# Another order of the same steps in a planned RWKV-7 and SwiGLU kernel

## The chip, the core and the metric

The kernel runs on one core of one Trainium2 chip. The metric is device time in microseconds (us). The kernel before was run three times: 1099.3, 1105.6 and 1111.4 us, median 1105.6. One further execution was recorded by the hardware profiler; it took 1106.7 us from its first to its last instruction, and all figures of the profile are of that one.

## The reference

Two blocks follow each other. The first is a linear recurrence over 768 steps of a sequence, for 4 batches of 8 heads of width 40, each with a state of 40 x 40:

```
for t in range(S):
    y[:, :, t] = einsum('bhd,bhde->bhe', rt, state)
    Sa = einsum('bhde,bhe->bhd', state, at)
    state = state * wt[:, :, None, :] - einsum('bhd,bhe->bhde', Sa, bt) \
            + einsum('bhd,bhe->bhde', vt, kt)
```

The second takes the recurrence's output as 3072 tokens of width 320, divides each by its root mean square, scales it by `rms_g`, and applies a SwiGLU layer:

```
g, val = xn @ w_gate, xn @ w_val          # 320 x 1536 each
out = (g * sigmoid(g) * val) @ w_out      # 1536 x 320
```

The weights come as 64-bit floating point numbers and are used as fp32.

## The kernel before, in words

**Chunks.** The recurrence is cut into 24 chunks of 32 steps. `front(c)` (line 678) loads a chunk (`wan`, `kbn`, `VU`, `wn`), turns it over on PE (the tensor engine), and builds over the levels 1 to 16 the products of keys and decays (`K`, `Ab`, `KN`) and the chunk's triangular matrix `LT`. `LT` is written to `sB` in device memory and read back into `M` in another layout. `inverse(c)` (line 782) inverts it by 31 pairs of DVE (vector engine) steps, `tmp<-Yi,M` and `Yi<-Yi,tmp`, each of which needs the one before. The result goes to `sY` in device memory and back into `LT`. `main(c)` (line 802) uses `LT` in two `lower` products, updates the state `ST`, computes the chunk's output `y` level by level (`As`, `level`, `down`), and turns it into a column block of `xg`, the normalized input of the second block.

**Groups.** Two chunks make a group of 64 steps. `feed(g)` (line 924) is the SwiGLU layer for such a group of 256 tokens, with 12 slices of weights taken in six pairs. For each pair SP (the sync engine) loads two `wf` tiles, PE makes the products `h64` and `h`, ACT (the scalar engine) makes `sg`, DVE makes `hT`, and PE adds `out` into the PSUM tile `po`. ACT then copies `po` to `o`, and SP stores it. There are 12 groups.

**Weights.** `narrow` (line 958) turns the weights' 64-bit numbers into fp32 on DVE and ACT, once, and stores them in `sW`, from which all groups load. It runs beside the first chunks.

**Order.** Nothing is issued while these functions run. Each call of a helper (`dve` at line 473, `scalar` at 492, `dma` at 516, `pe` at 526) records a step in a `Plan`, with what it needs; a PE step is a whole product of up to 64 matmuls. When all is recorded, `Plan.issue` (line 347) walks through a written list, `ORDER`. A number in it picks a recorded step, counted from the first one that is not yet issued; a `-` issues one filler matmul (line 1002), which multiplies the identity by itself into an unused part of `po` to keep PE's clock up:

```
for word in order.split():
    if word == "-":
        self.order.append(None)
        self.warm()
        continue
    i = first + int(word)
```

So `ORDER` sets the sequence of steps on each of the five engines, DMA issues included: SP and GpSimd (POOL) issue loads in that sequence, and a load that must wait for its buffer holds up those behind it. `PAIRS` gives each of the 491 PSUM uses ("rooms") one of three pairs of banks. Waits between engines follow from the recorded needs and from the reuse of buffers and banks.

All steps of a helper bear that helper's line in the profile: L475 is nearly all of DVE, L521 all matmuls of products, L524 the turns, L518 all DMA issues, L502 ACT's copies, L1002 the filler. They are told apart by their tiles.

Of the kernel before, what the change touches and what calls it, by code (L numbers as in the profile page):

```python
# [16 lines left out]
P = 128  # L17
# [10 lines left out]
PRODUCTS = {  # L28
    "out": (0.915, 0.359, 0.434, 0, 2560), "h": (1.618, 0.306, 0.381, 0, 4096), "h64": (0.864, 0.2, 0.2, 1, 2048),
    "turn": (0.824, 0.2, 0.273, 0, 2048), "turn3": (0.278, 0.3, 0.275, 0, 768), "turn4": (0.388, 0.249, 0.272, 0, 1024),  # L30
    "turny": (0.46, 0.145, 0.248, 2, 640), "gram": (0.927, 0.124, 0.264, 2, 512), "gramk": (0.927, 0.158, 0.263, 2, 1792),
    "score": (0.927, 0.138, 0.243, 2, 1024), "level": (0.603, 0.132, 0.216, 5, 1024), "state": (0.597, 0.126, 0.245, 3, 640),
    "lower": (0.594, 0.126, 0.216, 4, 320), "update": (0.603, 0.154, 0.265, 2, 1280), "y0": (0.613, 0.132, 0.236, 2, 1024),
}

LOADS = {
    "sB": (1.75, 0.1), "LT": (2.0, 0.2), "M": (2.67, 0.44), "sY": (1.96, 0.3), "wf": (4.02, 1.46), "r": (4.25, 0.69),
    "tok": (2.09, 0.27), "wn": (2.36, 0.31), "wan": (2.68, 0.51), "out": (1.9, 0.15), "g": (2.37, 0.68),
    "raw2": (3.1, 0.75), "raw64": (2.21, 0.27), "rawo": (2.9, 0.7), "rawp": (2.4, 0.3), "sW": (1.5, 0.7),
}  # L40
# [5 lines left out]
36 33 2 26 42 1 31 0 25 343 37 29 107 38 24 36 26 34 262 2 13 1 35 40 0 190 24 339 13 14 - - - 40 17 44 15 41 43 55  # L46
42 8 60 47 175 72 48 45 84 185 59 68 186 585 54 58 - - - - - 49 93 586 53 179 69 71 599 81 176 57 597 50 67 178 609
70 188 80 622 51 92 16 623 65 610 52 56 177 633 64 66 - - - - - - - - - - - - 61 189 9 598 77 79 187 78 587 620 62 0
587 81 - - - - 72 75 179 82 62 90 595 384 194 588 87 11 633 89 589 74 395 620 197 590 380 88 73 195 391 - - - - 101
196 209 390 610 84 102 214 381 201 611 202 5 212 86 213 383 591 85 0 222 92 591 611 17 95 221 224 223 384 94 234 225  # L50
- - 197 233 237 93 391 245 246 592 328 393 198 598 645 612 0 641 598 15 612 592 - 338 205 206 380 642 599 209 0 207
612 200 0 337 612 186 598 6 326 613 2 599 641 34 176 200 216 217 23 600 389 215 33 201 355 95 202 177 96 214 - - - -
211 187 339 93 0 577 0 561 578 297 579 171 192 53 187 191 - - - 182 188 200 623 172 185 625 186 580 562 581 612 355
582 199 1065 197 583 611 183 198 624 184 0 152 1005 850 298 0 298 0 837 295 0 0 0 83 130 298 148 0 298 83 0 507 307
833 0 303 555 0 840 307 0 290 0 67 125 316 314 0 132 125 67 0 0 131 314 0 286 325 0 130 0 298 130 0 291 292 - - - -
- 287 0 293 0 304 0 316 305 301 0 0 283 0 296 0 311 0 322 281 0 286 0 295 280 0 292 - - - - - - - - - - - - - - - -
- 288 0 0 0 0 301 0 285 62 301 116 305 0 283 250 116 0 - - - - - - - - 293 0 258 112 296 0 110 300 256 0 308 307 245
293 292 0 0 304 0 288 0 301 - - - - - - 298 306 0 0 313 0 297 0 0 0 293 310 494 301 0 494 0 302 0 0 299 492 0 0 296
0 246 0 791 0 0 0 787 0 0 93 468 2 796 94 469 0 94 462 794 0 467 93 94 290 461 95 462 96 468 511 97 469 291 98 470
481 289 99 292 471 0 99 100 101 471 102 472 103 481 511 104 482 105 488 106 489 107 483 2 490 108 109 0 293 109 490  # L60
0 108 0 0 379 0 379 387 0 387 369 0 405 378 387 406 0 - - - - - - - - - - - - - - - - - - - - - - - - - - - - - - -
- - - - - - - - - - - - - - - - - - - - - - - - - - - - - - - - - - - - - - - - 44 0 367 377 0 415 0 42 0 414 383 43
412 0 383 410 0 383 40 373 0 0 0 0 0 0 36 0 377 - - - - - - - - - - - - - - - - - 44 0 377 35 44 0 414 0 0 82 0 32 -
43 0 373 0 90 0 229 407 38 88 0 40 78 226 42 38 41 47 48 0 43 226 42 50 45 48 396 0 50 396 43 0 396 0 0 379 395 380
0 395 380 0 401 0 394 0 378 242 400 44 0 400 47 0 145 45 377 242 0 145 391 377 0 216 1 145 391 42 635 398 429 626
146 0 397 39 145 426 634 398 146 147 631 43 623 44 621 45 632 46 148 47 622 - - - - 639 375 376 149 48 416 239 641
830 150 399 377 640 840 0 150 641 653 48 838 151 658 152 645 828 - - - - - - 642 153 670 154 646 155 682 49 656 50
156 669 657 51 157 666 158 667 52 159 643 668 - - - - - - - 53 389 160 161 678 162 1 651 652 - 647 2 702 655 3 654 0
594 610 611 609 625 595 636 109 608 110 596 373 - - - - - - - - - - - 605 590 374 111 345 783 607 626 782 383 112
627 620 622 385 793 113 623 606 375 382 114 792 621 - - - - - - - 617 384 115 376 346 116 377 619 117 635 634 118  # L70
618 378 119 - - - - - 160 633 120 379 121 163 380 161 122 381 123 162 124 164 386 - - - - - - - - - 629 125 387 126
127 128 388 129 630 130 640 631 389 638 131 390 - - - - - 167 641 132 391 133 639 134 392 168 135 393 - - - - - 165
136 394 137 138 430 139 166 571 431 581 643 140 - - - 171 721 644 580 141 642 142 570 143 174 645 144 173 145 178 -
- - 182 175 146 177 147 172 150 149 179 - - - 180 148 637 176 185 732 432 186 433 0 1065 584 283 - 39 1064 36 582 38
284 638 37 40 635 583 0 17 635 480 625 567 497 40 18 624 498 41 284 568 626 42 285 499 627 43 570 286 642 636 44 500
2 706 287 45 643 897 0 493 500 501 643 287 897 656 644 648 2 45 597 907 502 649 494 0 457 860 458 0 613 0 457 611
552 0 - 596 457 621 598 0 622 0 456 595 610 853 457 622 458 634 854 0 505 - - - 500 360 765 521 361 449 531 519 764
504 532 543 362 508 363 0 500 517 543 501 4 515 363 502 364 506 419 514 365 5 366 516 367 0 367 419 368 421 369 370
420 422 44 0 370 - 430 371 44 0 3 40 0 367 426 368 369 370 504 371 37 372 373 374 375 429 376 526 525 521 377 505
522 0 338 466 390 339 397 377 9 340 391 341 392 342 430 393 398 343 480 440 400 378 439 395 387 429 396 394 403 408  # L80
388 0 403 0 342 474 700 403 578 0 700 403 342 709 490 343 0 474 7 696 405 343 709 475 403 344 0 487 706 472 0 485
695 10 343 704 404 0 404 0 4 404 37 405 0 401 31 337 481 402 45 0 474 3 337 338 41 339 402 0 42 3 0 398 705 399 471
50 335 400 898 336 703 470 401 337 37 907 338 339 402 27 480 699 908 704 340 403 341 897 479 486 701 889 343 700 584
478 890 713 714 481 899 702 719 28 706 559 900 342 712 29 560 731 30 0 531 9 0 9 683 684 17 10 0 10 454 0 450 552 10
451 0 10 672 0 672 - - - - - - - - - - - - - - - - 662 25 0 27 670 26 0 682 680 24 695 539 677 676 678 704 661 37 -
- - - 3 36 675 662 296 4 681 434 691 663 679 692 703 672 5 0 0 428 1 680 683 42 682 666 43 687 681 667 20 40 686 21
677 695 2 22 292 0 675 705 287 0 675 287 688 0 671 0 669 665 269 7 17 410 8 682 29 411 412 30 667 413 414 0 8 665 0
675 8 681 672 9 674 0 9 672 - - - - - - - - - - 481 0 9 37 483 411 0 471 0 25 5 401 6 402 403 404 471 7 39 405 473 -
- - - - - - - - - - - 16 0 0 28 8 27 397 0 397 28 0 397 0 654 462 0 5 396 36 8 397 398 37 399 14 47 462 15 0 457 10
723 44 3 11 43 458 583 644 21 12 646 582 4 13 645 461 0 571 21 13 572 458 393 22 14 394 15 466 0 391 455 19 0 372 0  # L90
16 436 0 694 28 5 27 442 6 695 371 439 7 0 696 0 451 370 435 6 760 0 745 0 428 0 741 362 425 0 751 433 362 741 0 748
362 0 425 423 358 733 0 358 0 744 358 432 359 360 0 427 428 0 7 359 0 359 15 0 359 360 6 0 425 0 428 442 359 360 361
362 363 364 0 360 361 742 362 0 362 363 364 419 365 742 366 367 2 368 423 751 369 370 371 372 373 424 675 374 7 0
424 2 0 1154 672 0 1154 421 422 732 432 738 0 669 730 1002 732 670 420 995 731 439 742 685 985 421 0 993 421 687 735
422 686 743 4 1002 423 748 736 991 424 746 983 366 757 367 759 368 425 992 369 744 0 369 746 371 757 755 370 759 768
# [155 lines left out]
02120120011200000212212111011122220122021022212000000011220202110212200222211102110020200221100000001111122201220111  # L251
201121210102011022201201201
"""


class Piece:

# [136 lines left out]
def kernel(  # L394
# [41 lines left out]
    N = 8  # L436
# [98 lines left out]
    ident = const.tile([P, P], FP32, name="ident")  # L535
# [499 lines left out]
```

## Time and profile before

| What | Value |
|---|---|
| median of 3 runs | 1105.6 us |
| profiled execution, span | 1106.7 us |
| PE busy, filler included | 1032.9 us (93%) |
| filler alone | 75.7 us, 560 records |
| DVE busy | 907.4 us (82%), 3065 instructions |
| ACT busy | 453.9 us (41%) |
| POOL busy | 302.7 us (27%) |
| DMA | 145.4 MB, 131 GB/s on average |
| granted PE clock, mean | 0.984 |

Busy time is the union of an engine's instructions. The row of PE holds matmuls only; weight loads overlap them and have a row of their own. A row of a group of instructions gives their number, busy time, mean duration in ns, and the idle time of the engine just before them with what ended it. A row of the waits gives who waited for whom, the total in us, how often, and the longest. A row of DMA issues gives the KB of each and the median time from issue to landing in us. A row of a stretch gives its bounds and length in us, then for each engine the busy time and, in brackets, the instructions.

### The profile page before, as it was taken

The numbers are of one execution on the slowest core, as the hardware profiler recorded it, in microseconds if no ns is written. First come the engines' busy times: TensorE is split into PE (matmuls) and PEld (weight loads), VectorE is DVE, ScalarE is ACT, GpSimd is POOL, SyncE is SP. The second block draws the span as 40 slices with busy tenths as digits, with TensorE's granted clock in tenths as the row PEclk, the third lists the DMA queues.
The fourth block names the chain that finished last, engine by engine and source line by source line (L and its number), as shares of the span: only waits on it lengthen the run. The fifth ranks groups of instructions, "written<-read, shape, count | busy, mean of one in ns | idle before, by whom it ended". The sixth has DMA issues, their size and how long they took to land.

```text
span 1106.7 us, 53122 instructions
## 1 busy us (share of the span) xinstructions
PE 1032.9 (93%) x23152; PEld 852.5 (77%) x23152; DVE 907.4 (82%) x3065; ACT 453.9 (41%) x989; POOL 302.7 (27%) x534
## 2 busy tenths in 40 slices
PE   5697888989999999999999999999989999999998
PEld 4597877767778877877777877887878878787876
DVE  5998999799889888798789789988898889798421
ACT  3644544654244344344344345334335435332211
POOL 7520342122233223223323323413404312200000
PEclk9789899989999999999999999999999999999999
DMA  7545453786555536456535545645636546434242
GB/s 158 134 85 164 122 125 85 198 240 165 124 141 124 149 80 160 117 125 141 150 101 138 138 123 134 154 101 151 139 95 166 125 112 147 108 108 131 80 141 80
DMA packets 171177, 145.43 MB, mean 131 GB/s; under 512 B 123712, under 2 KB 142080, under 8 KB 170944
## 3 DMA queue, kind: packets, MB, share of 16 engines
q1 hardware_dynamic: 152576, 119.06, 39.8%
q0 software_dynamic: 16192, 22.64, 11.0%
q8 instruction: 182, 2.98, 1.2%
q10 hardware_dynamic: 2176, 0.33, 0.2%
q14 instruction: 51, 0.42, 0.1%
HBM read 125.83 MB, written 16.12 MB: 128 GB/s over the span
## 4 chain that ended last, share of the span: by engine, by line
PE 59%; DVE 19%; issue 7%; ACT 3%; DMA 3%; POOL 2%; SPq 0%; DVEq 0%; POOLq 0%; ACTq 0%
PE ps L521 41%; PE po L521 11%; PE ps L524 7%; DVE LT L475 3%; DVE tmp L475 3%; DVE Yi L475 2%; DVE As L475 2%; DVE y L475 2%; DVE K L475 1%; DVE hT L475 1%; DVE r L475 1%; DVE ex L475 1%; DVE wf L475 1%; ACT K L502 1%; DMA sB<-LT 1%
## 5 line engine op out<-in xcount | busy, mean ns | idle before, releaser
L521 PE MATMUL ps<-xg,wf 128*128 128x256 f32 (+1 forms) x1728 | 354.5, 392 | 3.1 <-DVE xg L475 2.1
L521 PEld LDWEIGHTS ps<-xg,wf 128*128 128x128 f32 (+1 forms) x1728 | 261.3, 189 | 58.4 <-issue 14.3
L521 PE MATMUL po<-wf,hT 128*128 128x320 f32 x576 | 178.8, 444 | 3.2 <-DVE hT L475 1.8
L475 DVE TENSOR_TENSOR tmp<-Yi,M 128x60 f32<-128x60 f32 (+24 forms) x744 | 156.0, 210 | 18.1 <-DMA M<-sB 1.9
L475 DVE TENSOR_TENSOR Yi<-Yi,tmp 128x60 f32<-128x60 f32 (+24 forms) x744 | 155.3, 209 | 15.9
L518 POOL DMA_DIRECT2D VU<-in_v_dram x92 | 53.4, 587 | 356.6 <-PE ps L524 206.3
L498 ACT ACTIVATE sg<-ps 128x256 f32<-128x256 f32 x144 | 53.7, 383 | 236.4 <-PE ps L521 225.0
L521 PEld LDWEIGHTS po<-wf,hT 128*128 128x128 f32 x576 | 102.2, 190 | 39.3 <-issue 3.7
L475 DVE TENSOR_TENSOR hT<-ps,sg 128x256 f32<-128x256 f32 x144 | 59.3, 419 | 54.7 <-ACT sg L498 53.4
L475 DVE TENSOR_TENSOR K<-K,T 128x512 f32<-128x512 f32 (+1 forms) x192 | 93.4, 495 | 8.7 <-PE ps L521 3.4
L521 PEld LDWEIGHTS ps<-Ab,K 40*64 40x64 f32 x4608 | 76.6, 137 | 30.8 <-issue 9.6
L521 PE MATMUL ps<-Ab,K 40*64 40x56 f32 x4608 | 86.4, 223 | 11.5 <-DVE K L475 3.1
L502 ACT COPY K<-K 128x256 f32<-128x256 f32 (+1 forms) x168 | 71.2, 443 | 61.9 <-PE ps L521 40.6
L475 DVE TENSOR_TENSOR As<-ps,msi 128x256 f32<-128x256 f32 (+1 forms) x192 | 83.2, 481 | 10.6 <-PE ps L521 10.4
L502 ACT COPY KN<-ps 128x640 f32<-128x640 f32 x96 | 66.4, 691 | 53.4 <-PE ps L524 20.7
L521 PEld LDWEIGHTS ps<-As,KN 128*40 128x40 f32 x3072 | 67.2, 125 | 19.5 <-issue 11.7
L521 PE MATMUL ps<-As,KN 128*40 128x32 f32 x3072 | 74.5, 206 | 7.3 <-issue 4.6
L1002 PE MATMUL po<-ident 128*128 128x128 f32 x560 | 75.7, 291 | 5.3 <-ACT po L544 5.3
L1002 PEld LDWEIGHTS po<-ident 128*128 128x128 f32 x560 | 70.4, 203 | 6.7 <-POOL wan L514 5.2
L518 POOL DMA_DIRECT2D kbn<-in_b_dram x92 | 53.6, 586 | 78.5 <-PE ps L521 70.8
L518 POOL DMA_DIRECT2D wn<-in_w_dram x92 | 51.5, 566 | 85.9 <-DVE tmp L475 32.4
L518 POOL DMA_DIRECT2D kbn<-in_k_dram x92 | 53.4, 584 | 75.7 <-PE ps L521 75.0
(124 smaller groups left out, 1529.2 us busy)
## 6 DMA issues: line engine op xcount, KB each, us to landing
wf<-sW SPq DMA_DIRECT2D x144, 480.0 KB, 4.2
M<-sB SPq DMA_DIRECT2D x96, 128.0 KB, 3.9
rn<-in_r_dram SPq DMA_DIRECT2D x24, 160.0 KB, 4.3
sW<-ex SPq DMA_DIRECT2D x16, 240.0 KB, 4.0
out_dram<-o SPq DMA_DIRECT2D x48, 80.0 KB, 3.5
kbn<-in_b_dram POOLq DMA_DIRECT2D x92, 40.0 KB, 3.2
wan<-in_w_dram POOLq DMA_DIRECT2D x46, 80.0 KB, 3.9
wan<-in_a_dram POOLq DMA_DIRECT2D x46, 80.0 KB, 4.3
```

The source lines that it names most:

```text
L475: plan.add("DVE", time + more + each * size(o), 0.087, lambda at: fn(at(o), *m(at)), [o], aps(*args))
L498: scalar(o, [a], lambda at: nc.scalar.activation(at(o), at(a), f, **kw), aps(acc), 0.1 if f in (AF.Square, AF.Relu) else 0.0)
L502: scalar(o, [a], lambda at: nc.scalar.copy(at(o), at(a)), extra=more)
L518: plan.add(by, 0.6 if by == "POOL" else 0.45, 0.0, lambda at: queue.dma_start(out=o, in_=i), [o], [i], load=LOADS[load], since=since)
L521: return o, lhsT, rhs, lambda at: nc.tensor.matmul(at(o), lhsT, rhs, start=start, stop=stop, skip_group_check=True), 4
L524: return o, i, ident, lambda at: nc.tensor.transpose(at(o), i, ident), 2
L1002: plan.warm = lambda: nc.tensor.matmul(po_[:, 0, DM:DM + P], ident, ident, start=False, stop=False, skip_group_check=True)
```

## The change

`ORDER` and `PAIRS` are replaced. The same steps with the same tiles and operands are issued in another sequence, found anew by exchanging steps along the chain that ends last: 3,043 on DVE, 968 on ACT, 897 on PE, 712 on SP and 507 on POOL. A DVE step moves by 16 places at the median and by 257 at most. 315 of the 491 rooms lie in another PSUM pair. The number of fillers goes from 280 to 235. The tables `PRODUCTS` and `LOADS`, which held durations for the planner and took no part in the issue, are gone, and with them their uses; a PE step records its kind instead, and one kind of turn gets a name of its own.

```
-PRODUCTS = {
-    "out": (0.915, 0.359, 0.434, 0, 2560), "h": (1.618, 0.306, 0.381, 0, 4096), "h64": (0.864, 0.2, 0.2, 1, 2048),
...
-LOADS = {
-    "sB": (1.75, 0.1), "LT": (2.0, 0.2), "M": (2.67, 0.44), "sY": (1.96, 0.3), "wf": (4.02, 1.46), "r": (4.25, 0.69),
...
 ORDER = """
-36 33 2 26 42 1 31 0 25 343 37 29 107 38 24 36 26 34 262 2 13 1 35 40 0 190 24 339 13 14 - - - 40 17 44 15 41 43 55
...
+36 27 3 26 37 1 346 345 0 184 26 17 39 29 21 37 36 2 3 27 44 12 38 6 28 194 108 183 45 46 182 51 190 52 - - - - 48
...
-        plan.add(by, 0.6 if by == "POOL" else 0.45, 0.0, lambda at: queue.dma_start(out=o, in_=i), [o], [i], load=LOADS[load], since=since)
+        plan.add(by, 0.6 if by == "POOL" else 0.45, 0.0, lambda at: queue.dma_start(out=o, in_=i), [o], [i], load=load, since=since)
...
-        time, drain, tail, mode, area = PRODUCTS[kind]
-        plan.add("PE", time, tail, issue, [s[0] for s in steps] + more, [x for s in steps for x in s[1:3]],
-                 drain=drain, mode=mode, area=area, many=sum(s[4] for s in steps))
+        plan.add("PE", 0.0, 0.0, issue, [s[0] for s in steps] + more, [x for s in steps for x in s[1:3]],
+                 kind=kind, many=sum(s[4] for s in steps))
...
-        pe("turn", [flip(ps[0:outs, at(n), 0:ins], t[0:ins, n, 0:outs], ident[0:ins, 0:ins]) for n in range(N)])
+        pe("turn" if ins == P else "turnS", [flip(ps[0:outs, at(n), 0:ins], t[0:ins, n, 0:outs], ident[0:ins, 0:ins]) for n in range(N)])
```

## The prediction

> **What bounds the kernel now.** I read the busy time by stretches first. I cut the span where feed group 0 starts (165 us), where group 1 starts (270) and where the last group starts (1060).
>
> ```profile
> core 0: us, PE busy (x) PEld busy (x) DVE busy (x) ACT busy (x) POOL busy (x), PEclk, DMA share, GB/s
> 0.00:165.00 165.00, 129.85 (x2860) 118.90 (x2864) 142.21 (x469) 82.04 (x162) 67.80 (x134) 0.92 0.56 132
> 165.00:270.00 105.00, 93.91 (x2023) 76.95 (x2013) 94.26 (x294) 55.01 (x111) 26.30 (x45) 0.97 0.62 169
> 270.00:1060.00 790.00, 767.90 (x18093) 625.61 (x18092) 665.52 (x2293) 311.37 (x705) 208.60 (x356) 1.00 0.51 128
> 1060.00:1107.00 47.00, 41.28 (x192) 30.99 (x192) 5.46 (x13) 5.44 (x14) 0.00 (x0) 0.98 0.37 111
> ```
>
> PE looks busy throughout, but part of it is the filler matmul of L1002, which does no work. The same two first stretches for that line alone:
>
> ```profile
> 0.00:165.00 165.00, 65.05 (x474) 60.24 (x474) 0.92 0.56 132
> 165.00:270.00 105.00, 10.64 (x86) 10.14 (x86) 0.97 0.62 169
> ```
>
> Taking filler off, PE works 64.8 of the first 165 us, 83.3 of the next 105, 767.9 of the next 790. It loses 100, 22, 22 and 6 us: two thirds before the first feed step. There DVE is the busy one: it starts its first planned step at 14.9 us, and from then to 165 its idle stretches longer than 0.12 us add up to 8.1 us. So **the first 270 us go by DVE, the 790 us behind them by PE**, and a new order can gain most in front.
>
> Next the order in time of DVE, in the middle stretch (start, duration, instruction):
>
> ```profile
> 337.56 0.19 DVE L475 TENSOR_TENSOR tmp<-Yi,M 128x35 f32<-128x35 f32 x1
> 337.78 0.20 DVE L475 TENSOR_TENSOR Yi<-Yi,tmp 128x35 f32<-128x35 f32 x1
> 338.01 0.19 DVE L475 TENSOR_TENSOR tmp<-Yi,M 128x28 f32<-128x28 f32 x1
> 338.12 0.41 DVE L475 TENSOR_TENSOR y<-y,ps 128x256 f32<-128x256 f32 x1
> 338.56 0.42 DVE L475 TENSOR_TENSOR y<-y,T 128x256 f32<-128x256 f32 x1
> ```
>
> A step that reads what its neighbour just wrote starts after it has ended (337.56 + 0.19 = 337.75, next at 337.78). A step that doesn't starts before (338.01 + 0.19 = 338.20, next at 338.12). Over all 1,168 dependent neighbours of this trace the median gap is +0.035 us, over the 1,874 others -0.082. **Two dependent DVE steps side by side cost 0.117 us more than the same two apart.**
>
> **The change, part by part.** No instruction goes but filler: 3,043 DVE, 897 PE, 968 ACT, 712 SP and 507 POOL steps stand in both lists.
>
> *PE's own work.* With each step at its median start-to-start time behind that kind, by the next kind, the sum is 942 us in the old order and 940 in the new. I cost it at 0.
>
> *Filler.* 280 become 235; at 0.27 us each (75.7 us for 560 records, two to a filler) that is 12.2 us less. They stood where PE had nothing else, so 0 by themselves. If PE then idles and its clock falls (it was granted 0.92 in the first stretch), the 64.8 us of work there grow; at 0.80 by 64.8 x (0.92/0.80 - 1) = 10 us. I take 0, since DVE ends last there, and keep 10.
>
> [...]
>
> *DVE's order.* Counting dependent neighbours in the two built lists gives 1,168 before and 792 after. 376 x 0.117 = 44 us of DVE time go. What that is worth depends on the place. I summed, in order, the duration of each DVE step's form, plus 0.035 or minus 0.082 by its neighbour, up to four points, and the PE work standing ahead of the PE step that uses the result. Where DVE sets the pace, the time won is the fall in DVE ahead, less what PE has done less by then:
>
> - group 0 starts: DVE 134.7 to 123.7 (100 dependent neighbours become 38: 7.3 us, and 3.7 us of work less ahead), PE ahead 59.5 to 58.4: 11.0 - 1.1 = 9.9 us
> - group 0, third weight pair: DVE 174.8 to 154.3, PE 90.8 to 84.3: 14.0 us
> - group 0, last weight pair: DVE 222.7 to 216.1, PE 129.2 to 136.5: 6.6 + 7.3 = 13.9 us
> - group 1 starts: DVE 227.5 to 209.5 (178 dependent become 52), PE 137.7 to 130.6: 10.9 us
>
> The four are alike, mean 12.2. **I take -12 us up to 270 us.** The ends are -18 (all of the DVE fall) and 0 (the loads are late instead).
>
> [...]
>
> *The middle.* DVE's sum per group falls from 72.6 to 69.6 us, against 81 us that a group takes, so DVE isn't the bound there. What can go is PE's 22 us of idle. PE's waits from 300 to 1060 us:
>
> ```profile
> PE ps L521 <- issue: 5.5, 12, 1.3
> PE ps L521 <- DVE LT L475: 3.0, 5, 1.4
> PE ps L521 <- ACT KN L502: 1.5, 4, 0.6
> PE ps L521 <- DVE xg L475: 1.5, 2, 1.0
> PE ps L524 <- DVE tmp L475: 1.3, 2, 0.9
> ```
>
> The rows that name DVE add up to 8.5 us. I take two thirds, **-6 us**, since new places of steps also make new waits; the ends are 0 and -22. The last product for the state (main 23, 0.75 us), whose result nobody reads, now stands behind everything, beside the copy of `o` (0.69 us) and the last store: 0.
>
> *Round trips through SP.* The inverse leaves the core and comes back (`sY`, then `LT`); the step that waits is `lower` on PE, with the rest of that chunk behind it.
>
> ```profile
> wf<-sW SPq DMA_DIRECT2D x144, 480.0 KB, 4.2
> ...
> LT<-sY SPq DMA_DIRECT2D x96, 32.0 KB, 2.9
> ```
>
> In the trace, from the last `Yi` to the landing of the last `LT` it took 9.9 us at best (chunk 23), 15.5 at the median, when the order left time. The old order has at least 14.0 us of PE work in that place from chunk 2 on. The new one has 9.4 (chunk 2), 9.1 (3), 11.2 (4), 10.0 (14), 11.2 (17) and 7.1 (23). At 9.9 us the shortfall is 0.5 + 0.8 + 2.8 = **+4 us**, which I take, because the SP queue need not carry the slack it carried. The ends are 0 and, at 15.5 for all 22 chunks, +43. Loads of `wf` with under 6 us of cover rise from 6 to 17 of 144; 4.2 us is their median landing: 0. The trip of `LT` to `M` gets shorter too (7.7 us of PE work at chunk 13, where the fastest start of an inverse came 10.2 us behind `LT`), but DVE waits there, with 11 us to spare per group: 0, and up to 2 us a chunk if PE runs dry.
>
> **Sum:** -12 - 6 + 4 = -14 us on the execution of 1106.7 us: 1092.7. The runs' median lies 1.1 us below that execution, so 1091.5.
>
> **The rivals.**
>
> *No gain.* The order was found against costs that the chip doesn't have, and where DVE leaves off ACT or a load is late: DVE waited 9.6 us for ACT's copy of `T` at the start already. Then the 12 us shrink to 4 or less and the new waits take that back: 1106.7 - 4 + 4, about 1106.
>
> *Slower: the round trip of the inverse.* `lower` stands at the head of PE's queue, so each late `LT` stops everything. If a trip takes 14 us in the new order, the shortfalls are 4.6 + 4.9 + 2.8 + 4.0 + 2.8 + 6.9, and 1.2 in two further chunks: 27 us. With the 12 won in front and nothing in the middle: 1106.7 - 12 + 27 = 1122. From about 12 us a trip it takes back what was won (14 us); from some 13.5 the kernel is over 1% slower. For it: landings spread up to 5 us at the ninth decile. Against it: 9.9 was reached.
>
> *A larger gain.* DVE's 18 us count in full and most of the 22 in the middle go: 1106.7 - 18 - 18 + 1 = 1072.
>
> **How the numbers follow.** Forecast (1080 to 1098) 0.47, larger gain 0.12, no gain 0.26, slower 0.15. A measurement of this kernel tells about 1%, 11 us (its runs spread from 1099 to 1111). Below 1094.5 lie the larger gain and most of the forecast: 0.56; within 0.29; slower 0.15. Half of the larger gain (0.06) and nearly all of the slower case (0.13) are left out: 1072 to 1114.
>
> **What would show it.** Right: the first step of feed group 0 starts near 155 us and group 1 near 258; DVE has some 790 neighbours with the longer gap; PE idle from there to the last group is below 20 us; 470 filler records. Wrong: PE waits named after `LT<-sY` of over a microsecond in many chunks, group 0 still at 165, or a lower clock in front with PE on the chain.

## The result, and the profile after

The changed kernel takes 1204.3 us (median of four runs, 1193.9 to 1205.7) against 1104.2 us (1099.3 to 1111.4) for the kernel before: a ratio of 1.088, 95% interval 1.082 to 1.094. It is 8.8% slower where a gain of about 1% was forecast. The profiled execution takes 1203.6 us with a span of 1201.8 us.

First the busy time by stretches of the changed kernel, cut where its groups 0, 1 and 11 start. The columns are those shown of the kernel before: bounds, length, busy time of PE, its weight loads, DVE, ACT and POOL, granted clock, DMA share, GB/s.

```profile
core 0: us, PE busy (x) PEld busy (x) DVE busy (x) ACT busy (x) POOL busy (x), PEclk, DMA share, GB/s
0.00:150.00 150.00, 117.04 (x2777) 108.22 (x2778) 132.19 (x451) 77.72 (x156) 65.55 (x129) 0.95 0.56 140
150.00:257.00 107.00, 90.89 (x1971) 72.56 (x1969) 85.70 (x278) 53.23 (x107) 25.41 (x42) 0.90 0.55 149
257.00:1153.00 896.00, 803.79 (x18058) 644.52 (x18060) 648.35 (x2327) 303.86 (x712) 214.50 (x363) 0.97 0.44 115
1153.00:1202.00 49.00, 43.47 (x260) 31.95 (x258) 4.81 (x12) 5.78 (x14) 0.00 (x0) 0.98 0.36 113
```

The front is shorter, as forecast. The long stretch behind it took 790 us before and takes 896 now, and PE, with as many instructions in it (18,058 against 18,093), is busy 36 us longer there and idle 70 us longer. Its clock, 1.00 before, is 0.97. DVE does the same work in less time (665.5 before, 648.4 now).

Next PE's waits of the changed kernel from 300 us to the last group: what it waited for, total us, how often, the longest.

```profile
PE ps L522 <- issue: 26.6, 23, 4.4
PE ps L522 <- DVE hT L476: 8.9, 14, 1.7
PE po L522 <- DVE hT L476: 8.4, 7, 2.4
PE ps L522 <- DVE tmp L476: 7.1, 4, 3.9
```

Two things are new beside the rows shown of before. "Issue", a wait for nothing that the profile shows, was 5.5 us with 1.3 at the longest; now it is 26.6 with 4.4. And PE waits for `hT`, DVE's step of the feed, which was not among its five largest waits. The loads did not take longer from issue to landing (4.2 and 2.9 us before):

```profile
wf<-sW SPq DMA_DIRECT2D x144, 480.0 KB, 3.9
...
LT<-sY SPq DMA_DIRECT2D x96, 32.0 KB, 2.9
```

**What an "issue" wait is.** In the order in time of PE it lies in the middle of a product, where nothing is handed over. This is one product of 64 matmuls of the changed kernel (start, duration, instruction, number of them, and in brackets the idle time ahead):

```profile
356.28 0.90 PE L522 MATMUL ps<-A,K 40*64 40x56 f32 x43
361.55 0.89 PE L522 MATMUL ps<-A,K 40*64 40x56 f32 x21 [4.37 <-issue]
```

I counted PE's instructions (matmuls, weight loads, and the waits on semaphores that stand between them) from the start of the trace. Nearly all of these stalls sit where the count leaves 193 when divided by 256, in every run of this study. The queue q8, of the kind "instruction" in the page, moved 181 packets of 16,384 bytes in this trace, in which I count 46,432 instructions of PE, and 182 in that of before, with 46,625: one packet for 256 instructions. I read this as PE at the end of a piece of its code while the next piece is not there yet: the packet ahead of the stall above started at 358.6 us and took 1.5 us, and PE went on 1.5 us after it had landed. In all traces the fetch of a piece started when PE had at most 297 instructions left (the median is about 177), took about 1.1 us, and the first instruction ran at least 1.1 us after it landed (1.3 to 1.5 us in the 28 stalls of this trace behind 270 us). By estimate from the rows of this trace, 256 instructions of PE last some 28 us in `h` products (two of them, 32 instructions, in 3.5 us) but 2.3 us in products of `Ab` and `K` (128 in 1.16 us). I call these stalls **late code**.

The table gives, for each kernel, group starts from the traces and two sums behind 270 us: stalls of more than 0.15 us at these boundaries, and the time in which PE's granted clock was at half ("half clock"). At half clock the `h` matmuls of the changed kernel stood 0.43 us apart, start to start at the median of 16, and 0.22 us at full clock. "`sg` late" sums, over the 144 `sg` steps, the time from the end of the product it reads to its start.

| kernel | time, us | group 0 | group 1 | group 2 | group 11 | late code, us (number) | half clock, us | `sg` late, us |
|---|---|---|---|---|---|---|---|---|
| before | 1104.2 | 165.5 | 270.1 | 346.2 | 1060.6 | 8.7 (16) | 3 | 62 |
| after | 1204.3 | 150.5 | 257.3 | 362.4 | 1152.7 | 34.1 (28) | 55 | 193 |
| front1 | 1139.8 | 154.1 | 276.0 | 353.1 | 1095.7 | 19.8 (24) | 30 | 73 |
| rest1 | 1215.3 | 163.1 | 267.3 | 357.8 | 1163.4 | 37.5 (33) | 75 | 174 |
| noM | 1189.3 | | | | | 33.4 (28) | 44 | 189 |
| noall | 1220.5 | 157.9 | 265.0 | 364.7 | | 43.2 (36) | 80 | 186 |
| noW | 1168.4 | 150.5 | 256.6 | 356.8 | 1117.5 | 15.1 (18) | 33 | 190 |
| noWB | 1098.3 | | | | | 2.0 (4) | 2 | 62 |
| shiftA | 1218.6 | 161.4 | 264.7 | 364.9 | 1167.4 | 40.7 (35) | 64 | 188 |
| shiftB | 1153.9 | 165.4 | 271.5 | 353.5 | 1106.0 | 30.9 (28) | 46 | 62 |
| shiftB256 | 1112.8 | 168.3 | 274.3 | 350.5 | 1064.8 | 9.8 (16) | 4 | 61 |
| shiftBW | 1134.7 | 166.0 | 273.3 | 352.0 | 1086.6 | 14.3 (17) | 36 | 62 |
| front1fix | 1113.6 | 149.7 | 273.7 | 349.9 | 1063.4 | 7.4 (14) | 3 | 75 |
| front1fill | 1115.8 | 152.8 | 278.0 | 354.1 | 1067.9 | 7.8 (14) | 2 | 73 |
| adjB | 1137.7 | 161.6 | 269.4 | 349.8 | 1088.2 | 11.3 (17) | 15 | 152 |
| early | 1208.3 | 151.8 | 258.1 | 363.5 | 1157.6 | 32.6 (32) | 50 | 114 |

The kernel before took 1103 to 1106 us (medians) beside every group of runs. Where no interval is given, a kernel was run once.

### The profile page after: what moved, and what is told of

It reads as the page before. It is cut to its first block, busy times and chain, and to the rows that moved or that the text cites. A ratio compares the mean times of both kernels' runs of the same rounds, so it can differ in the third digit from the quotient of the medians.

```text
span 1201.8 us, 52799 instructions
## 1 busy us (share of the span) xinstructions
PE 1055.2 (88%) x23062; PEld 857.2 (71%) x23062; DVE 871.1 (72%) x3065; ACT 440.6 (37%) x989; POOL 305.5 (25%) x534
## 5 line engine op out<-in xcount | busy, mean ns | idle before, releaser
L522 PE MATMUL ps<-xg,wf 128*128 128x256 f32 (+1 forms) x1728 | 363.7, 401 | 19.2 <-issue 5.2
L522 PEld LDWEIGHTS ps<-xg,wf 128*128 128x128 f32 (+1 forms) x1728 | 268.2, 195 | 78.8 <-issue 25.0
L522 PE MATMUL po<-wf,hT 128*128 128x320 f32 x576 | 189.1, 460 | 13.2 <-DVE hT L476 11.2
L522 PEld LDWEIGHTS po<-wf,hT 128*128 128x128 f32 x576 | 105.6, 197 | 53.0 <-DVE hT L476 16.1
L476 DVE TENSOR_TENSOR As<-ps,msi 128x256 f32<-128x256 f32 (+1 forms) x192 | 87.4, 482 | 9.1 <-PE ps L522 8.8
L476 DVE TENSOR_TENSOR y<-y,ps 128x256 f32<-128x256 f32 x119 | 49.8, 418 | 18.1 <-PE ps L522 15.3
L1002 PE MATMUL po<-ident 128*128 128x128 f32 x470 | 62.4, 290 | 0.0
```

Source lines behind the costliest of these rows:

```text
L476: plan.add("DVE", time + more + each * size(o), 0.087, lambda at: fn(at(o), *m(at)), [o], aps(*args))
L522: return o, lhsT, rhs, lambda at: nc.tensor.matmul(at(o), lhsT, rhs, start=start, stop=stop, skip_group_check=True), 4
L1002: plan.warm = lambda: nc.tensor.matmul(po_[:, 0, DM:DM + P], ident, ident, start=False, stop=False, skip_group_check=True)
```

## The experiments

**Which part of the order costs, and is it the round trips?** The first four kernels ask this. front1 takes the new order for its first 1,455 steps, up to the first PE step of group 1, and the old order for the steps that are left; rest1 is the reverse (1,520 steps of the old order).

```
front1:  ORDER = new order up to feed 1, then the remaining steps in the old order
rest1:   ORDER = old order up to feed 1, then the remaining steps in the new order
```

> New order up to the step that opens feed group 1 (257 us in the new profile, 270 in the old), then the old order of all that is left. If the new order's front is a true gain and all loss lies behind it: about 1106.7 - 13 = 1094 us. If the front only borrowed (steps put off that cost later): 1105 or more. A loss from the filler that is missing in front would show here too: over 1110.

> Old order up to the step that opens feed group 1, then the new order of the rest. If the loss lies in the new order's rest whatever stands in front: about 1202 + 13 = 1215 us. If it is a debt from the new front: under 1130.

front1 took 1139.8 us (ratio 1.0285, 1.0238 to 1.0331), rest1 1215.3. The new rest alone is worse than the whole change, so the loss comes from behind group 1. But front1 is slower too, though the steps behind group 1 are in the old order; that pointed away from the steps themselves.

noM lets the inverse read the identity in place of `M`; noall also lets `lower` read it in place of `LT`, and the turns and `KN` in place of `wan`, `kbn` and `wn`. All loads are still issued, but no step on PE, DVE or ACT waits for these. Both leave the recurrence's real data out.

```
-            tt(tmp, Y[...].to_broadcast((P, n, m)), M[:, i:i + 1, i + 1:].to_broadcast((P, n, m)), MUL)
+            tt(tmp, Y[...].to_broadcast((P, n, m)), ident[:, None, i + 1:C].to_broadcast((P, n, m)), MUL)
...
-        pe("lower", [mm(X[...], LT[own(i, n), o * N + slot(n)], VU[...], ...
+        pe("lower", [mm(X[...], ident[own(i, n), 0:C], VU[...], ...
```

> New order; the inverse reads a constant in place of M, so that it no longer waits for the trip LT to sB to M (the loads still run; the inverse of the true matrix is left out). Theory of the round trips (too little cover for DMA): this trip alone has 40 us of the chain behind 270 us, so 1160 to 1180. Theory of the handoffs on the core (PSUM pairs, DVE to PE and back): 1195 or more. Theory of the clock (PE at half speed in 60 us): 1195 or more, unless the stalls that slow the clock go with it.

> New order; the inverse reads a constant in place of M, both lower products read the identity in place of LT, and the chunk's turns and KN read the identity in place of wan, kbn and wn, so that no round trip and no chunk load stands in the way of a step (all DMAs still run; the recurrence is left out). Round trips: the whole loss goes, 1085 to 1115 us. Handoffs on the core: 1160 or more. Clock: 1170 or more.

noM took 1189.3 us, 15 less than the changed kernel. DVE's wait for `M`, in the changed kernel

```profile
DVE tmp L476 <- DMA M<-sB: 20.7, 8, 5.4
```

is gone, so the trip of `LT` to `M` was worth up to about 15 us; part of it may be the clock, with 11 us less at half, and the single run lies only 5 us below the fastest of the changed kernel. noall took 1220.5. With nothing waiting for the round trips and these loads the kernel is no faster, so **the round trips are not the main cause**. Its late code rose to 43 us and its half clock to 80, which led me to these two columns.

**Late code.** Theory F: PE runs through a piece of code quickly while the fetch of the next waits behind the packets of loads; the stalls then drop PE's clock to half. Its rival H: the handoffs between the engines are too tight. noW and noWB cut the largest load to a fifteenth, from group 2 on, in the new and the old order.

```
-                dma(wf, sW[f + e], "wf")
+                dma(wf if g < 2 else wf[:, 0:P // 2], sW[f + e] if g < 2 else sW[f + e][:, 0:P // 2], "wf")
```

> The new order, but from feed group 2 on each load of `wf` brings 64 of its 960 columns (32 KB in place of 480); the products run on the weights that the tile held before, so the output of those groups is left wrong. Theory F (late code): PE stands still in the middle of products, always at a boundary of 256 of its instructions, because the fetch of its next 16,384 bytes of instructions waits behind the packets of loads, of which `wf` has half the time; stalls of 1 to 4 us then drop PE's clock to half. It expects the stalls at these boundaries to fall from 34 us behind 270 us to under 15, the half-clock time there from 55 us to under 20, and 1115 to 1145 us. Theory H (handoffs: the new order leaves each step too little time between engines): the loads of `wf` are not what is late, so 1180 to 1205 us.

> The same cut of the `wf` loads in the old order, as the control. Both theories: PE is the bound behind 270 us and loses 20 us there, 9 of them at the boundaries; 1090 to 1106 us.

noW took 1168.4 us, between the two forecasts: late code fell to 15 us, half clock only to 33. noWB took 1098.3, as expected. So the loads of `wf` do delay the code (34 us of late code with them, 15 with the short ones), but 70 us lie between the two kernels even so. Late code is one cause of at least two.

shiftA and shiftB move all boundaries by half a piece, with 32 more fillers in the first 96 us.

```
 ORDER: every fourth of the first 128 fillers twice, "-" -> "- -"
```

> The new order with 32 more fillers among those of the first 90 us, where PE waits anyway: 128 more instructions, which shifts every later boundary of 256 instructions by half a piece of code. Theory F: the stalls move to 128 instructions from where they were, other steps are hit, and the sum stays as it is if the order makes them (1185 to 1215 us); if only the chance position of the boundaries makes them, it falls below 1160. Theory H: 1195 to 1210, with the stalls between the same steps as before.

> The old order with the same 32 more fillers in the first 90 us. If the old order is good only by the chance position of its boundaries, over 1130 us. If its order makes it safe (theory F by order, or theory H), 1100 to 1115.

shiftB is the surprise: the old order, with nothing changed but 32 fillers in a stretch where PE waits, takes 1153.9 us. Its late code is 31 us, near that of the new order. shiftA took 1218.6, 4 us above the range for stalls that the order makes, so the new order is bad at both positions. The waits of PE behind 270 us, here of shiftB:

```profile
PE ps L519 <- issue: 30.9, 28, 3.1
```

If the place of the boundaries is what counts, another 32 fillers must bring the old time back, since behind the last of them the boundaries then lie where they lay. And front1 must be cured by 45 fillers: it has 235 where the old order has 280, so its steps behind group 1 lie 180 instructions off.

```
shiftB256:  64 more fillers in the first 230 us of the old order
front1fix:  45 more fillers in the first 235 us of front1
```

The expectations say "in the first 90 us"; in the kernels as they ran, 33 of the added fillers of each stand in the first 96 us and the others behind, the last at 230 and 235 us. The sums of the table begin at 270 us, behind all of them.

> The old order with 64 more fillers in the first 90 us: 256 more instructions, so that every later boundary of the code lies again where it lay in the old order. Theory F (late code, and the old order is good only where its boundaries lie): with half a shift the old order took 1154 us; with the whole one the stalls at the boundaries behind 270 us fall from 31 back to under 14 us, the half-clock time there to under 10, and the time to 1103 to 1118 us (64 fillers are 17 us of PE, in a stretch where PE waits). If more fillers were what cost the 48 us, twice as many cost more: over 1154.

> The kernel that follows the new order up to group 1 and the old one behind it (1140 us) has 45 fillers fewer than the old order, so all its later steps lie 180 instructions from where the old order has them. Here 45 fillers are added in the first 90 us; nothing else. Theory F: the boundaries behind group 1 are back in the old places, the stalls there fall from 20 to under 12 us, half clock from 30 to under 10, and the time to 1090 to 1110 us. If the new front itself harms what follows, or the seam of the two orders does: 1130 to 1150.

The same row in shiftB256 and in front1fix:

```profile
PE ps L519 <- issue: 6.2, 11, 0.9
```

```profile
PE ps L520 <- issue: 4.7, 10, 1.2
```

shiftB256 took 1112.8 us and front1fix 1113.6 (ratio 1.0091, 1.0062 to 1.0120); in both the late code and the half clock are back at the old values. Twice the fillers cost less than half of them: **the position of the code boundaries is shown to be worth 41 to 48 us to the old order** (1153.9 against 1112.8 and, beside it, 1106.2). front1fix missed its range by 4 us at the upper end; what its front costs is taken up below.

A calculation fits this. For each boundary I took the time that PE needs for the 297 instructions ahead of it, without the stalls, and asked by how much it falls short of the fetch delays of the same trace, for sixteen positions of the boundaries. In the old order the sum is 10 us where the boundaries lie, 9 at the best position and 21 at half a piece away, the worst. In the new order it is 28 to 32 at every position. It is a calculation, not a run; it says that the old order sits almost at its best place, and that the new one has no such place.

shiftBW joins the two conditions: the boundaries of shiftB, the short `wf` loads of noW.

> The old order with its boundaries shifted by half a piece of code (1154 us), and from feed group 2 on only 64 of the 960 columns of each `wf` loaded; the products of those groups run on older weights, so their output is left wrong. Theory F says that a boundary costs time only where two things meet: PE runs through a piece of code quickly, and the fetch of the next waits behind loads. With the loads cut, the stalls at the boundaries behind 270 us fall from 31 to under 12 us, the half clock there from 46 to under 15, and the time to 1100 to 1120 us, near the unshifted old order with the same cut (1098). If the shift costs in another way than through late fetches: 1135 to 1154.

PE's four largest waits behind 270 us in shiftBW:

```profile
PE ps L519 <- issue: 14.3, 17, 2.3
PE ps L519 <- DVE xg L473: 2.2, 3, 1.0
PE ps L519 <- ACT KN L500: 2.2, 3, 0.8
PE ps L519 <- DVE LT L473: 2.1, 3, 1.4
```

It took 1134.7 us, a miss, and only 0.3 us short of the range for a shift that costs in another way. Late code fell from 31 to 14 us, half of the way, but the half clock stayed at 36, and the time is midway. Beside noWB, the unshifted order with the same cut, it is 36 us slower, with 12 us more late code and 34 us more half clock, in which PE does some 17 us less work (an estimate from the 0.43 and 0.22 us above): together 29 of the 36. In shiftB the mean busy share of the DMA engines while a fetch was due was 0.37 for fetches that started under 1.5 us after the earliest moment, and 0.61 for those over 4 us. In the changed kernel it was 0.35 and 0.53, and 0.60 for those between, so the load on the DMA engines is not all that sets the delay. Nor is late code all that lowers the clock: ahead of the two longest falls of shiftBW (10.2 us from 545.8 and 13.7 us from 835.9 us) it was 0.5 of 1.6 us and none of 2.1 us of PE's pauses in the 7.5 us before, and the other pauses were waits for DVE and ACT. Why the clock fell there stays open.

**The feed's handoff.** What else is in the new order? Here is a weight pair of the kernel before, on PE and ACT: an `h` product, the product behind it, and `sg`.

```profile
458.06 1.99 PE L521 MATMUL ps<-xg,wf 128*128 128x256 f32 x8
...
459.98 0.81 PE L521 MATMUL ps<-As,KN 128*40 128x32 f32 x32
460.09 0.38 ACT L498 ACTIVATE sg<-ps 128x256 f32<-128x256 f32 x1 [0.95 <-PE ps L521]
```

`sg` starts 0.04 us after its product has ended. And one of the changed kernel, where the two `h` products of the pair follow each other (16 matmuls in one row):

```profile
605.03 3.72 PE L522 MATMUL ps<-xg,wf 128*128 128x256 f32 x16
```

```profile
608.79 0.38 ACT L499 ACTIVATE sg<-ps 128x256 f32<-128x256 f32 x1 [2.19 <-PE ps L522]
```

The first product was over at 607.0; `sg` starts when the second has ended, 1.76 us later. In all 33 pairs of the new order that stand like this, and in all 14 of the old one, `sg` does not start before the end of the second. Both products write the same PSUM banks, in other columns. In the built program 56 `sg` steps of the new order, and 21 of the old, wait for a later count of PE's semaphore than that of their own product. Theory B: this wait is a cost that no step of mine contained. I tested it from both sides. adjB puts it into the old order; early takes it out of the new one, without a change of any engine's own sequence, by listing the readers of a PSUM pair ahead of the next product into it.

```
adjB:   ... h(e=0)  x  h(e=1) ...          ->  ... h(e=0)  h(e=1)  x ...          (27 pairs, old order)
early:  ... h(e=0)  h(e=1)  sg(e=0) ...    ->  ... h(e=0)  sg(e=0)  h(e=1) ...    (34 steps, new order)
```

> The old order, but in 27 of the 72 weight pairs the second `h` product is moved forward, directly behind the first; nothing else moves. Theory B (wait of the feed): the first `sg` of a pair cannot start before the second `h` has ended when that one was listed ahead of it, since both are in the same PSUM banks; the new order has this 33 times, the old one 14. It expects 41 cases of 1.7 us and over, `sg` late behind its product by about 130 us in all in place of 62, and, by replaying the order with the median durations of the steps, 27 us more: 1125 to 1150 us, as far as the clock holds. If ACT and DVE have time for it: 1100 to 1112.

> The new order with the same sequence of steps on each engine; only in the common list 34 steps that read a PSUM pair now stand ahead of the next product into the same pair, where they stood behind it. Theory B: `sg` then starts with its own product (late by under 130 us in all, from 193), but now PE's second `h` waits for `sg`, because the banks are kept apart as a whole: PE has some 20 new waits of about 0.5 us for ACT, and the time doesn't fall (1195 to 1220). If `sg`'s lateness alone cost the time and PE need not wait: 1170 to 1185.

adjB took 1137.7 us, 33 more than the old order, with `sg` late by 152 us (60 cases of 1.7 us and over, more than the 41 expected, since steps queued behind are late too). Its half clock is 12 us longer and its late code 2.6, some 9 us in all; the other 25 are near the 27 that the expectation's replay gave for the wait. early took 1208.3. There `sg` starts at once, but now PE waits, on the same products as above:

```profile
608.31 1.99 PE L519 MATMUL ps<-xg,wf 128*128 128x256 f32 x8
...
610.34 0.38 ACT L496 ACTIVATE sg<-ps 128x256 f32<-128x256 f32 x1 [0.47 <-PE ps L519]
...
610.78 3.07 PE L519 MATMUL ps<-xg,wf 128*128 128x256 f32 x13 [0.47 <-ACT sg L496]
```

```profile
PE ps L519 <- ACT sg L496: 23.4, 34, 2.6
```

The last row is from PE's waits over early's whole span: 23.4 us in 34 waits for `sg`, a row that the changed kernel's list does not show. Both expectations held. Two neighbouring `h` products of one pair cost either ACT and DVE 1.8 us or PE about 0.5 us (0.7 in the mean of the 34 waits). early only moves the wait, so no run here has the new order without it, and what would come of that is not shown; its size there rests on the replay below.

**How the two add up.** I replayed each order with every step's median duration at full clock from the traces of before and after, letting a step start when its engine's earlier step, its inputs and its PSUM pair allow. This is a computation; against the traces' own ends, with each kernel's own durations put in, it is 15 us too long for the old order and 6 too short for the new one.

| | before | after | difference |
|---|---|---|---|
| median durations, no waits for the PSUM bank | 1101.0 | 1079.6 | -21.4 |
| with these waits | 1102.2 | 1110.9 | +30.1 of it from the waits |
| and each kernel's own step durations | 1122.5 | 1194.4 | +63.2 of it from these |
| end in the trace | 1107.0 | 1200.9 | +93.9 |

Nearly all of the third line comes from PE's own steps, which hold the late code and the half clock: alone they make 81 of the 83 us in the new order. The order by itself, as the forecast counted it, gains 21 us. Some 22 us of the difference stay unassigned. The runs give a rough second count: of the 70 us between noW and noWB, 13 are late code, some 16 are lost in 31 us more of half clock, and 30 are the waits by the replay, which leaves 11.

**Where the front's gain goes.** front1fix starts group 0 at 149.7 us, 15.8 earlier than the old order, and group 1 at 273.7, 3.6 later. Its stretches:

```profile
0.00:150.00 150.00, 121.23 (x2860) 112.78 (x2862) 130.96 (x449) 78.15 (x157) 65.23 (x129) 0.99 0.56 139
150.00:274.00 124.00, 100.51 (x2012) 79.41 (x2012) 94.52 (x315) 55.24 (x117) 30.15 (x50) 0.88 0.56 150
```

Between groups 0 and 1 PE's clock is 0.88 (0.97 before), with half clock for 31 us against 7 before. front1fill adds 64 fillers at nine places where PE waited there.

```
ORDER of front1fix: 3 to 11 more "-" ahead of nine PE steps between 156 and 271 us
```

> The new order up to group 1 with the old boundaries behind it (1114 us), and 64 more fillers at the nine places between 150 and 274 us where PE waited for another engine. In that kernel PE's clock was at half for 31 of these 124 us (7 in the old order). If the fall of the clock is what takes back the front's gain, the half clock there falls below 15 us; the fillers themselves cost 8 us by the replay with median durations, so 1100 to 1112. If the order of the front is the cause whatever the clock: 1116 to 1128.

It took 1115.8 us; the half clock fell only to 20 us. This is inconclusive: the fillers took about as much as the better clock gave. That the clock takes back the front's gain is likely but not shown.

No kernel here that does all of the work beats the one before.

## Why the prediction was wrong

**The reading of the old profile held.** DVE sets the pace of the first 270 us and PE behind it. The rows say so, and the old order replayed with median durations ends at 1102.

**DVE's order: right in mechanism and size.** In the trace after there are 792 dependent neighbours with a median gap of +0.034 us and 2,250 others with -0.082; DVE's busy time fell from 907.4 to 871.1 us. Group 0 starts at 150.5 us (155 forecast), group 1 at 257.3 (258 forecast). But "**I take -12 us up to 270 us**" was taken as a gain to keep. The sum itself counted 7.1 us of PE work that the new order has not done by then, and in front1fix, where the old order's rest has to make it up, nothing is left of it at group 1.

**"PE's own work ... I cost it at 0" is the step that failed most.** The sum of median durations, 942 and 940 us, is right and says nothing about the durations that are not the median. In the old trace their excess is small because its code boundaries lie well (8.7 us of late code behind 270 us, 31 in shiftB); in another order of PE's steps they need not (28 to 32 us at every position of the new order, by the calculation above). This step should have read the 12 waits "PE ps L521 <- issue", which I quoted, as a cost that depends on the order. Its counterpart, 34 us of late code and 55 us at half clock behind 270 us, makes most of the 63 us in the table above.

**Filler at 0.** The 10 us kept for the clock were meant for the first stretch alone. In front1 the 45 fillers that went cost by moving every later boundary by 180 instructions: with them put back it is 26 us faster (1139.8 to 1113.6). The changed kernel has no such cure as far as the runs go (shiftA, 1218.6). How much idle time it takes to lower the clock is not shown. In the changed kernel's trace the half clock behind 270 us comes in pieces of 3.4, 6.8 and 10.2 us, but for the last at the end of the span, and ahead of the fall at 383.9 us pauses over 0.15 us add up to only 1.2 us in 7.5 us.

**The middle, -6 us with the ends 0 and -22.** The ends left out a loss. I wrote that "new places of steps also make new waits" and took a third off for it, without looking for one. The wait of `sg` and then `hT` for the second `h` product could be read in the old trace, in its 14 neighbouring pairs; the new order has 33. All waits for the PSUM bank together cost 30 us by the replay; 27 such pairs more cost 33 us in adjB, part of it by the clock. In the waits of DVE from 300 us on, the row of `hT` went from 17.2 to 49.3 us; the first line is of before, the second of after:

```profile
DVE hT L475 <- ACT sg L498: 17.2, 23, 2.4
```

```profile
DVE hT L476 <- ACT sg L499: 49.3, 37, 6.6
```

**The round trips, +4 us, and the slower rival.** The rival on the slower side named the wrong place. `lower` hardly waits for `LT` in the trace after (1.2 us for `LT<-sY` in the whole span), and noall without these trips is not faster. A smaller error is in "DVE waits there, with 11 us to spare per group: 0": the trip of `LT` to `M` turned out to cost up to about 15 us (noM).

**What the forecast could not have settled:** where the boundaries of the new order's code fall is fixed once it is built, but that PE runs into them at all showed in the old trace only as 8.7 us behind 270 us. That the old order owes over 40 us to their position was found only by the shift. Of the signs named, neither long waits for `LT<-sY` nor a late group 0 appeared, though the clock between groups 0 and 1 was lower (0.90); what did tell was the idle time of PE behind group 1, 92 us where under 20 was the sign of being right. (A slip that changes nothing: 1092.7 less 1.1 is 1091.6.)

## What to carry to other kernels

When PE runs many short matmuls, a wait that the profile puts down to "issue" in the middle of a product deserves a count of PE's instructions, its waits on semaphores included. Here the stalls shared one remainder, 193 of 256, and 32 more fillers, 128 PE instructions, changed the time by 4% (1106.2 to 1153.9 us) without touching the work; so an edit that adds or removes PE instructions ahead, fillers included, has to be suspected. A few fillers in an idle stretch at the start make a cheap test of it, and a control for every other change of order. And in a program built like this one a wait between engines is counted by the PSUM bank: two products into one bank, back to back, made the reader of the first wait for both (1.76 us in the pair shown), or the second product wait for the reader (0.7 us in the mean of the 34 waits of early).

## What was not expected of the hardware

- PE's instructions came in packets of 16,384 bytes, one for 256 instructions (181 for 46,432 in the changed kernel, 182 for 46,625 in the one before), and PE outran them: single stalls of up to 4.4 us, 34 us in all behind 270 us in the changed kernel. Fetches that started late went with busy DMA engines: in the trace of before their mean busy share was 0.32 during waits under 1.5 us and 0.70 during waits over 4 us, in the changed kernel 0.35 and 0.53; with short `wf` loads the new order's late code fell from 34 to 15 us.
- Such stalls stood ahead of most falls of PE's clock: for 7 of the 11 falls behind 270 us in the changed kernel, at least half of PE's idle time in the 7.5 us before the fall was late code. In the old order there is no fall behind 270 us but at the very end, and in shiftBW the longest fall has no late code ahead of it. That the stalls lower the clock is likely from this, not shown.
- A shift of the boundaries by 128 instructions took the old order from 1104 to 1154 us, and a shift by 256 brought it back to 1113.
